# Top-k attention, SwiGLU and experts on one core: other staging rooms for the f64 weights, queries transposed unsplit, and routing in four batches

## The chip, the cores and the metric

The kernel runs on one core of a Trainium2 chip. The metric is device time in microseconds (us); lower is better. An engine is named as the profile names it: PE multiplies matrices (PEld loads its stationary operand), DVE is the vector engine, ACT the scalar engine, POOL the GpSimd engine, SP the queue from which most transfers are issued. PSUM holds what PE writes.

## The reference, cut to what matters

```python
# 1. attention, q k v: (4, 8, 576, 64) f32; only the 32 largest scores of a row count
scores = q @ k.T / 8
scores = where(scores >= kth_largest(scores, 32), scores, -1e9)
x = softmax(scores) @ v                      # -> 2304 tokens x 512
# 2. SwiGLU block; its three weight matrices come as 8-byte doubles
xn = x / rms(x) * rms_g
x = (silu(xn @ w_gate) * (xn @ w_val)) @ w_out          # 512 -> 1536 -> 512
# 3. one expert of eight per token
logits = x @ w_gate2 + modality_bias[modality_id]
e = argmax(logits); p = softmax(logits)[e]
out = p * (relu(x @ w1[e]) @ w2[e])                     # 512 -> 1024 -> 512
```

## The kernel before, in words

The program has two parts. `front` does attention, the SwiGLU block (called the MLP here) and the routing; then, after a short hand-over through DRAM, the experts run one after another. Nothing of the second part is touched.

**Attention** runs in 72 steps of two tiles (128 query rows against 576 keys each). In a step, PE multiplies q by k (`qk`, tile `ps`), DVE finds the 32nd largest of each row with repeated MAX8 and MATCH_REPLACE8 (`topk`, tile `w`), ACT and POOL make the softmax in place (tile `s`), PE transposes it (`tr`: tile `pt`, and once per step the 64 left-over keys of both tiles in tile `sm`) and multiplies by v (`av`). A number in f32 is carried as a pair, a rounded part and the rest ("hi" and "lo").

**The query path before.** `dma_q` loads the raw rows of a step into `qr` six steps ahead. `split_q`, four steps ahead, has POOL make the pair `qs` in two operations (L454, L455). `trans_q`, two steps ahead, has PE turn both parts of both tiles, four transposes of 128x128 (L463, tile `pq`), and ACT copies the result to `qS` in one go (L471, or L476 in the steps for left-over rows). `qk` of the step reads `qS`.

**The weights.** The doubles come in 36 chunks of 512 KB. A chunk is loaded raw, DVE turns it into f32 with three integer operations per piece (L277, L282, L286) in a PSUM tile `wp`, and ACT and POOL write the hi and lo halves into `wg`, `wv` or `wo` (L292 to L295). The 12 chunks of `w_out` come first and are staged in the still empty rooms of `wg` and `wv`. The 24 chunks of `w_gate` and `w_val` (columns in three parts, c0, c1 and c2, of eight chunks each) are staged in the ring of tag `h`, which holds three chunks at a time; a chunk's load waits until an older one is converted. The list `WS` names the step at which each chunk's conversion is written into the program: c0 at step 2, c1 at step 4, c2 at step 5. The `wp` tiles of these 24 come from the PSUM pool `ps_f`, which has two buffers and is also the MLP's.

**The MLP and the routing.** The 2304 tokens make 18 blocks of 128, grouped in 17 granules. When attention has finished a granule, `granule` gives its atoms: norm, transposes `px`, six products with `wg` and `wv` (48 matmuls each, tile `pf`), two with `wo` (36 each, tile `po`, with the routing logits in the last columns). `route` picks the expert of each token on DVE, and `rank` counts on PE (L866 to L868) and DVE at which place of its expert's list a token comes and scatters it there with POOL (L889): once per granule.

The order on each engine is set when the program is built: work is written in the order of the steps, and a scheduler with a model of the engines places each instruction; on the chip every engine runs its list strictly in order. SP, too, issues its transfers in list order, so a transfer that waits for its buffer holds those behind it.

## Time and profile before

| | before |
| --- | --- |
| median of 3 runs (range) | 1250.49 us (1248.81 to 1254.15) |
| the profiled execution | 1253.59 us |
| its span, first to last instruction | 1251.9 us |
| last `sm` transpose, end of attention on PE | 831.4 us |
| last product of the MLP | 929.2 us |
| first transpose of the experts | 948.3 us |

The span falls into four stretches: up to about 220 us the weights are converted beside attention; up to 831 us attention and MLP run together; up to 929 us PE works off the rest of the MLP; after a gap of 19 us the experts run to the end. "Busy" of PE is modelled from the starts of pipelined matmuls, so that a stretch at 99% is one in which PE always had something in flight.

### The profile page before, as it was taken

How to read it: one execution, taken by the hardware profiler on the slowest of the kernel's cores; microseconds unless marked ns; L12 is line 12 of the kernel's file. 1: busy time of each engine (PE TensorE's matmuls, PEld its weight loads, DVE VectorE, ACT ScalarE, POOL GpSimd, SP SyncE). 2: the span in 40 equal slices, each digit the busy share in tenths (PEclk: the TensorE clock that was granted, in tenths of full speed). 3: DMA queues.
4: the chain of work that ended last, by engine and by line, in shares of the span. 5: the costliest groups of instructions: out<-in, count | busy, mean ns of one | idle time of the engine just before them, and what ended most of it. 6: DMA issues, size and time to landing. Idle time of an engine off the chain costs nothing. (4 is left out here: it accounts for less than half of the span.)

```text
span 1251.9 us, 32217 instructions
## 1 busy us (share of the span) xinstructions
PE 1134.4 (91%) x12286; PEld 1038.2 (83%) x12286; DVE 925.4 (74%) x2885; ACT 832.3 (66%) x1757; POOL 736.2 (59%) x850
## 2 busy tenths in 40 slices
PE   6866777999999999999999999999975899999994
PEld 6855666888999999999899999999965789899893
DVE  8899999759999999999999999951214525454260
ACT  5868887777888888888888788763313535354260
POOL 7866766858767878876899667554325313221100
PEclk9866576989999999999999999999997899999997
DMA  9143312011000111100011000000007735553320
GB/s 292 51 128 83 98 43 81 13 44 39 20 17 11 33 37 47 26 9 17 20 32 42 25 17 2 11 11 11 10 21 263 264 113 189 185 186 102 103 87 19
DMA packets 68882, 87.63 MB, mean 70 GB/s; under 512 B 34386, under 2 KB 43734, under 8 KB 68696
## 3 DMA queue, kind: packets, MB, share of 16 engines
q1 hardware_dynamic: 60152, 63.66, 16.7%
q0 software_dynamic: 6320, 16.31, 3.9%
q10 hardware_dynamic: 2224, 5.25, 1.1%
q8 instruction: 109, 1.79, 0.6%
q14 instruction: 77, 0.63, 0.2%
HBM read 75.58 MB, written 10.92 MB: 69 GB/s over the span
## 5 line engine op out<-in xcount | busy, mean ns | idle before, releaser
L563 DVE MAX8 w<-w 128x8 f32<-128x296 f32 x576 | 249.9, 456 | 1.2
L597 POOL TENSOR_TENSOR s<-s,r 128x576 f32<-128x576 f32 x144 | 200.9, 1416 | 31.3 <-ACT r L593 31.1
L566 DVE MATCH_REPLACE8 w<-w 128x296 f32<-128x296 f32 x432 | 193.2, 450 | 0.0
L748 PE MATMUL pf<-xT,wg 128*128 128x128 f16 (+1 forms) x2448 | 172.0, 224 | 4.0 <-DVE T L877 2.6
L748 PE MATMUL pf<-xT,wv 128*128 128x128 f16 (+1 forms) x2448 | 167.7, 222 | 0.0
L528 PE MATMUL ps<-kS,qS 128*128 128x288 f32 x640 | 138.5, 346 | 24.1 <-DVE w L544 23.0
L748 PE MATMUL po<-wo,h 128*128 128x264 f16 (+1 forms) x1296 | 157.5, 275 | 0.9 <-ACT t L775 0.9
L748 PEld LDWEIGHTS <-wg 128*128 128x128 f16 x2448 | 148.2, 99 | 10.8 <-issue 4.6
L748 PEld LDWEIGHTS <-wv 128*128 128x128 f16 x2448 | 145.3, 98 | 4.3
L748 PEld LDWEIGHTS <-h 128*128 128x128 f16 x1296 | 122.0, 98 | 18.9 <-issue 1.4
L528 PEld LDWEIGHTS ps<-kS,qS 128*128 128x128 f32 x640 | 103.9, 215 | 27.4 <-ACT r L593 19.7
L1184 DVE SCALAR_TENSOR_TENSOR hl<-ph,hh 128x256 fp32r<-128x256 f32 x88 | 37.0, 421 | 117.9 <-ACT hh L1183 117.9
L1240 POOL DMA_INDIRECT out_dram<-o,idx x23 | 23.0, 1000 | 171.5 <-ACT o L1239 152.3
L601 ACT ACTIVATE s<-s,mbs 128x576 f32<-128x576 f32 x144 | 113.2, 788 | 14.0 <-POOL s L597 13.7
L593 ACT ACTIVATE r<-s,mbs 128x576 f32<-128x576 f32 x144 | 104.9, 779 | 18.3 <-POOL mbs L584 18.0
L623 PE MATMUL pt<-identr,s 128*128 128x128 f32 x576 | 98.4, 302 | 17.0 <-ACT s L601 15.8
L541 ACT COPY s<-ps 128x576 f32<-128x576 f32 x144 | 93.0, 646 | 23.6 <-PE ps L528 22.9
L1181 PE MATMUL ph<-xh,wh 128*128 128x256 f32 x352 | 100.2, 288 | 6.8 <-PEq L1293 6.3
L1181 PE MATMUL ph<-xl,wh 128*128 128x256 f32 x352 | 99.2, 283 | 0.0
L1181 PE MATMUL ph<-xh,wl 128*128 128x256 f32 x352 | 99.1, 283 | 0.0
L780 POOL TENSOR_TENSOR t<-u,t 128x512 f32<-128x512 f32 x54 | 70.5, 1305 | 48.0 <-ACT t L775 30.5
L669 PE MATMUL pt<-vs,pT 128*128 128x64 f16 (+1 forms) x1680 | 88.3, 198 | 7.5 <-POOL pT L637 5.8
(206 smaller groups left out, 2807.6 us busy)
## 6 DMA issues: line engine op xcount, KB each, us to landing
wr<-in_moe_w_dram SPq DMA_DIRECT2D x48, 512.0 KB
wst<-in_moe_w_gate_dram SPq DMA_DIRECT2D x24, 256.0 KB
wst<-in_moe_w_val_dram SPq DMA_DIRECT2D x24, 256.0 KB
wr<-in_moe_w_dram ACTq DMA_DIRECT2D x10, 512.0 KB
kr<-in_k_dram SPq DMA_DIRECT2D x32, 128.0 KB
vt<-in_v_dram SPq DMA_DIRECT2D x32, 128.0 KB
x_d<-xo SPq DMA_DIRECT2D x16, 256.0 KB
qr<-in_q_dram SPq DMA_DIRECT2D x112, 32.0 KB
```

Of the source, the lines that this page charges most:

```text
L528: nc.tensor.matmul(out=ps[:, a, 0:HS], lhsT=qS[i // 2][:, i % 2, j, o2:o2 + 128], rhs=kt[:, m, ks], start=(n == 0), stop=(n == len(ops) - 1),)
L541: nc.scalar.copy(out=s.rearrange("p (a k) -> p a k", a=2), in_=ps[:, :, 0:HS])
L563: steps.append(lambda: dve.max(lists[t][:, 8 * r:8 * r + 8], src[t] if r == 0 else dst[t]))
L566: steps.append(lambda: dve.match_replace(out=dst[t], in_to_replace=lists[t][:, 8 * r:8 * r + 8], in_values=src[t] if r == 0 else dst[t], i ...
L593: nc.scalar.activation(out=d["r"], in_=d["s"], func=AF.Relu, scale=-BIG, bias=d["mb"][:, 1:2])
L597: nc.gpsimd.tensor_tensor(out=d["s"], in0=d["s"], in1=d.pop("r"), op=OP.subtract)
L601: nc.scalar.activation(out=d["s"], in_=d["s"], func=AF.Exp, scale=SCALE, bias=d["mb"][:, 0:1], accum_out=d["rs"])
L623: nc.tensor.transpose(pt[:, c * 128:(c + 1) * 128], e[:, e0 + c * 128:e0 + (c + 1) * 128], ident)
L669: nc.tensor.matmul(out=av_[o:o + n], lhsT=l, rhs=r, start=(a == 0), stop=(a == len(ops) - 1))
L748: nc.tensor.matmul(out=out_, lhsT=l, rhs=r, start=(a == 0), stop=(a == len(ops) - 1))
L780: nc.gpsimd.tensor_tensor(out=t, in0=u, in1=t, op=OP.mult)
L1181: nc.tensor.matmul(out=pt, lhsT=l[:, fs], rhs=r[:, kk, :], start=(n == 0), stop=(n == 3 * KD - 1))
```

## The change

1. **Rooms.** The c0 chunks are staged in the parts of `wg` and `wv` that are meant for c1 and c2, as soon as `w_out` has left them. Five chunks of c1 are loaded before them, into the ring `h` (three), the MLP's `u` buffers and its `xT` buffer. Four more chunks go where c2 belongs, in four pieces each, and the last seven through the ring `h`. c0's `wp` tiles come from the pool `ps_t`, which is attention's. `WS` now has c0 at step 1, c1 at step 2 and c2 at step 3.
2. **Queries.** `dma_q` now comes four steps ahead and fills a wider `qr`, in which each raw row stands twice (the transfer repeats it). `split_q` is gone. PE turns the raw f32 tile, two transposes per step; ACT writes the rounded part into `qS` and a plain copy `qf`, and POOL subtracts, which gives the lo part of `qS`.
3. **Routing.** `route` and `rank` run four times, for 6, 6, 5 and 1 blocks, after granules 5, 10, 15 and 16 (counted from 0). Logits are collected in one tile per batch; `rank` counts within a batch with one more matmul per pair of blocks (40 in all, where one was).

```diff
+    ENDS = [NG // 3, 2 * NG // 3 - 1, NG - 2, NG - 1]
+    batches = [
+        [blk for g in range(lo + 1, hi + 1) for blk in granules[g][1]] for lo, hi in zip([-1] + ENDS[:-1], ENDS)
+    ]
...
+            elif i < KF + NC1:
+                r = third(1, 3, 2 * NC1)
...
+            elif i == KF + NC1 + 3:
+                ts = [mp.tile([128, WC // 2, 2], I32, name="wst", tag="u", bufs=UB) for _ in range(2)]
+            elif i == KF + NC1 + 4:
+                t = mp.tile([128, WC, 2], I32, name="wst2", tag="xT", bufs=1)
...
+            elif KF + NC1 + OWN <= i < KF + NC1 + OWN + 4:
+                r = third(2, 3, 16)
...
-            pool, tag = (ps_t, "pt") if i < KF else (ps_f, "f")
+            pool, tag = (ps_t, "pt") if i < KF + NC1 else (ps_f, "f")
...
-        WS, WAT = [-4] * 4 + [-1] * 8 + [2] * 8 + [4] * 8 + [5] * 8, -1
+        WS, WAT, W1 = [-4] * 4 + [-1] * 8 + [1] * 8 + [2] * 8 + [3] * 8, -1, 0
...
-            qr = ap_.tile([128, 2, D], F32, name="qr", tag="qr", bufs=QB)
+            qr = ap_.tile([128, 2, 2, D], F32, name="qr", tag="qr", bufs=QB)
...
+                    nc.sync.dma_start(out=qr[:, t], in_=src.unsqueeze(1).to_broadcast([128, 2, D]))
...
-            nc.gpsimd.tensor_tensor(out=qs[:, :, 0], in0=q2, in1=z, op=OP.add)
-            nc.gpsimd.tensor_tensor(out=qs[:, :, 1], in0=q2, in1=qs[:, :, 0].bitcast(F32), op=OP.subtract)
...
-            pt = ps_m.tile([128, 512], F32R, name="pq", tag="sm")
+            pt = ps_m.tile([128, 512], F32, name="pq", tag="sm")
             for t in range(2):
-                for j in range(2):
...
+                nc.tensor.transpose(
+                    pt[:, t * 128:(t + 1) * 128], qr[:, t].rearrange("p a d -> p (a d)"), ident
+                )
...
+                nc.scalar.copy(out=hi, in_=cut(src))
+                nc.scalar.copy(out=qf, in_=src)
+                nc.gpsimd.tensor_tensor(out=lo, in0=cut(qf), in1=hi.bitcast(F32), op=OP.subtract)
...
-                at(s - 6, lambda s=s: dma_q(s))
+                at(s - 4, lambda s=s: dma_q(s))
...
-            at(s - 4, lambda s=s: split_q(s))
...
-                        if j == nb - 1:
+                        if j == nb - 1 and gi in ENDS:
                             route()
...
-            return pre, hid, res, [rank()]
+            return pre, hid, res, [rank()] if gi in ENDS else []
```

On PE, where the MLP first gets long runs. Before, this is the piece after the 16th `sm` transpose; the last row is the first of 48 matmuls in a row (line numbers are those of the kernel before):

```order
L628 MATMUL sm<-identr,s 128x128
L423 MATMUL pk<-identr,ks 128x128
L669 MATMUL pt<-vt,pT 128x64 x8
L669 MATMUL pt<-vt,pr 128x64 x2
L463 MATMUL pq<-identr,qs 128x128 x4
L528 MATMUL ps<-kS,qS 128x288 x4
L419 MATMUL pk<-identr,ks 128x128 x4
L748 LDWEIGHTS wv_109
L748 MATMUL pf<-xT,wv_109 128x128
```

Now it is the piece after the 13th (lines are those of the changed kernel: L793 is the MLP's product, L667 `tr`, L490 the query transposes), and 47 matmuls with `wg` and 47 with `wv` follow:

```order
L572 MATMUL ps<-kS,qS 128x288 x4
L672 MATMUL sm<-identr,s 128x128
L490 MATMUL pq<-identr,qr 128x128 x2
L667 MATMUL pt<-identr,s 128x128 x8
L793 LDWEIGHTS wg_107
L793 MATMUL pf<-xT,wg_107 128x128
```

The MLP's first runs stand three steps earlier in PE's list. Up to the 72nd `sm` transpose PE's list holds 4847 of the 6192 MLP matmuls before and 5092 now.

On SP, the first transfers. Before, the queries of step 0 (`qr`) are third in the list:

```order
L264 DMA wg_107<-in_moe_w_out_dram 128x1024 x2
L373 DMA kr<-in_k_dram 128x256
L376 DMA kr<-in_k_dram 64x64
L373 DMA kr<-in_k_dram 128x256
L376 DMA kr<-in_k_dram 64x64
L443 DMA qr<-in_q_dram 128x64 x2
```

Now they come behind all of `w_out` and are followed by the loads of c1 and c0:

```order
L300 DMA wv_110<-in_moe_w_out_dram 128x1024 x2
L477 DMA qr<-in_q_dram 128x2x64 x6
L300 DMA wst<-in_moe_w_gate_dram 128x512 x8
L300 DMA wst_364<-in_moe_w_val_dram 128x512 x2
L300 DMA wg_107<-in_moe_w_gate_dram 128x512 x4
L300 DMA wg_108<-in_moe_w_gate_dram 128x512 x2
L411 DMA kr<-in_k_dram 128x256
L414 DMA kr<-in_k_dram 64x64
```

The first three steps' queries moved behind 12 chunks, and the third pair of key loads behind 16 weight pieces where it stood behind five.

On POOL, in the middle of attention, with `s<-s,r` the softmax and `t`, `h` the MLP. Before, each step has the two operations of `split_q`:

```order
L597 TENSOR_TENSOR s<-s,r 128x576 x2
L454 TENSOR_TENSOR qs<-qr,zero 128x2x128
L637 TENSOR_TENSOR pT<-pf,pT 128x512
L407 TENSOR_TENSOR ks<-kr,zero 128x9x64
L455 TENSOR_TENSOR qs<-qr,qs 128x2x128
L780 TENSOR_TENSOR t<-u,t 128x512
```

Now it has one, which needs PE's transposes and both of ACT's copies first (L641 is the softmax, L825 and L827 the MLP):

```order
L628 TENSOR_TENSOR mbs<-w,cst_66 128x6
L509 TENSOR_TENSOR qS<-qf,qS 128x2x128
L641 TENSOR_TENSOR s<-s,r 128x576 x2
L509 TENSOR_TENSOR qS<-qf,qS 128x2x128
L825 TENSOR_TENSOR t<-u,t 128x512
L651 TENSOR_SCALAR sums<-sums 128x2
L827 TENSOR_TENSOR h<-t,h 128x512
```

The operation moved from ahead of the transposes to between them and `qk`. Between the last query transpose of a step and its first `qk` matmul, PE's list now holds 3 to 320 matmuls, in the middle 150; 11 of the 72 steps have fewer than 40.

## Rows read from the trace of the kernel before

**Rows 1.** Page, its first part and the granted clock (busy us, share, count).

```profile
PE 1134.4 (91%) x12286; PEld 1038.2 (83%) x12286; DVE 925.4 (74%) x2885; ACT 832.3 (66%) x1757; POOL 736.2 (59%) x850
...
PEclk9866576989999999999999999999997899999997
```

**Rows 2.** Busy time by stretch: PE, PEld, DVE, ACT, POOL, granted clock, DMA share, GB/s.

```profile
0.00:30.00 30.00, 18.49 (x115) 17.90 (x116) 24.16 (x53) 18.29 (x36) 22.93 (x42) 1.00 0.92 296
100.00:150.00 50.00, 33.87 (x201) 28.56 (x200) 50.00 (x167) 40.24 (x85) 35.98 (x41) 0.57 0.32 88
150.00:200.00 50.00, 37.17 (x299) 32.59 (x299) 50.00 (x171) 42.16 (x91) 34.96 (x45) 0.71 0.22 63
300.00:825.00 525.00, 520.35 (x6987) 481.21 (x6988) 508.15 (x1744) 435.81 (x978) 402.82 (x472) 1.00 0.08 23
350.00:800.00 450.00, 447.05 (x6017) 413.45 (x6016) 433.88 (x1479) 377.20 (x847) 345.39 (x402) 1.00 0.09 24
```

**Rows 3.** The chain of waits, its first piece: start us, us, what.

```profile
1205.87 0.97 DMA out_dram<-o,idx
```

**Rows 4.** Timeline of PE: `sm` transposes 13, 16, 72 (start us, us, engine, line).

```profile
179.23 0.33 PE L628 MATMUL sm<-identr,s 128*128 128x128 f32 x1
...
219.82 0.35 PE L628 MATMUL sm<-identr,s 128*128 128x128 f32 x1
...
831.41 0.28 PE L628 MATMUL sm<-identr,s 128*128 128x128 f32 x1
```

**Rows 5.** Timeline of DVE: a converted piece and what follows it at once.

```profile
219.29 0.42 DVE L277 TENSOR_SCALAR wp<-wst 128x256 int32<-128x256 int32 x1
219.62 0.42 DVE L286 SCALAR_TENSOR_TENSOR wp<-wst,wp 128x256 int32<-128x256 int32 x1
...
5.31 0.69 DVE L282 SCALAR_TENSOR_TENSOR wp<-wg,wp 128x512 int32<-128x512 int32 x1
5.92 0.69 DVE L277 TENSOR_SCALAR wp<-wg 128x512 int32<-128x512 int32 x1
```

**Rows 6.** Timeline of PE after attention: dense runs of the MLP.

```profile
911.68 2.84 PE L748 MATMUL pf<-xT,wg 128*128 128x128 f16 x48
...
917.04 10.72 PE L748 MATMUL po<-wo,h 128*128 128x264 f16 x95
```

**Rows 7.** Groups of PE in 350 to 800 us: out<-in xcount, busy us, mean ns.

```profile
L748 PE MATMUL pf<-xT,wg 128*128 128x128 f16 (+1 forms) x1385 | 103.6, 225 | 2.4 <-DVE u L770 1.1 <-DVE T L877 0.9 <-ACT t L775 0.3
L748 PE MATMUL pf<-xT,wv 128*128 128x128 f16 (+1 forms) x1344 | 98.8, 225 | 0.0
L748 PE MATMUL po<-wo,h 128*128 128x256 f16 (+1 forms) x762 | 94.5, 275 | 0.0
L628 PE MATMUL sm<-identr,s 128*128 128x128 f32 x42 | 11.7, 278 | 0.0
```

**Rows 8.** Timeline of PE: runs of query and of softmax transposes at granted clock 1.00.

```profile
286.77 0.26 PE L463 MATMUL pq<-identr,qs 128*128 128x128 f32 x1
286.92 0.45 PE L463 MATMUL pq<-identr,qs 128*128 128x128 f32 x3
...
232.25 0.61 PE L623 MATMUL pt<-identr,s 128*128 128x128 f32 x4
281.80 1.04 PE L623 MATMUL pt<-identr,s 128*128 128x128 f32 x8
```

**Rows 9.** Groups of the whole span: transposes, copies and POOL operations.

```profile
L463 PE MATMUL pq<-identr,qs 128*128 128x128 f32 x288 | 43.2, 272 | 1.5 <-ACT qS L471 1.3 <-ACT kS L422 0.2
L623 PE MATMUL pt<-identr,s 128*128 128x128 f32 x576 | 98.4, 302 | 17.0 <-ACT s L601 15.8 <-ACT xn L678 0.8
L471 ACT CAST qS<-pq 128x512 fp32r<-128x512 f32 x64 | 39.2, 613 | 1.5 <-PE pq L463 1.4
L812 ACT ACTIVATE xo<-po 128x256 f32<-128x256 f32 x36 | 13.8, 388 | 26.9 <-DVE L L807 20.8 <-PE po L748 6.0
L454 POOL TENSOR_TENSOR qs<-qr,zero 128x256 fp32r<-128x256 f32 x72 | 44.4, 616 | 32.4 <-PE pq L463 31.5 <-PE pk L419 0.6
L455 POOL TENSOR_TENSOR qs<-qr,qs 128x256 fp32r<-128x256 f32 x72 | 52.5, 730 | 2.3
L597 POOL TENSOR_TENSOR s<-s,r 128x576 f32<-128x576 f32 x144 | 200.9, 1416 | 31.3 <-ACT r L593 31.1
```

**Rows 10.** Timeline of one routing after attention, DVE and PE (brackets: idle time, releaser).

```profile
902.46 0.16 DVE L840 TENSOR_REDUCE mx<-L 128x1 f32<-128x8 f32 x1
...
903.60 0.15 DVE L855 TENSOR_SCALAR gt<-gt 128x1 f32<-128x1 f32 x1
...
906.03 0.16 DVE L884 TENSOR_TENSOR acc_oh<-acc_oh,O 128x8 f16<-128x8 f16 x1 [1.25 <-PE pr L868]
...
906.83 0.14 DVE L887 COPY pay<-gt 128x1 f32<-128x1 f32 x1
...
906.32 2.84 PE L748 MATMUL pf<-xT,wg 128*128 128x128 f16 x48 [0.33 <-DVE T L877]
...
831.58 0.17 PE L867 MATMUL pr<-acc_oh,ones 128*128 128x8 f16 x1
831.61 0.17 PE L868 MATMUL pr<-O,tri 128*128 128x8 f16 x1
```

**Rows 11.** The first 30 us: SP and DVE timeline; DMA queue: packets, MB, share.

```profile
4.05 1.06 SPq L443 DMA_DIRECT2D qr<-in_q_dram  x2
...
14.83 2.50 SPq L264 DMA_DIRECT2D wv<-in_moe_w_out_dram  x5
...
19.04 0.45 DVE L543 TENSOR_TENSOR w<-s,ps 128x288 f32<-128x288 f32 x1
...
q1 hardware_dynamic: 60152, 63.66, 16.7%
```

**Rows 12.** Groups of the whole span: POOL's scatter of the routing.

```profile
L889 POOL DMA_INDIRECT tab_d<-pay,si x18 | 19.2, 1068 | 14.0 <-DVE pay L887 11.9 <-issue 1.4 <-DVE w L545 0.3
```

More of the change, by code (lines that the diff above doesn't have):

```diff
@@ L249, in weight_chunk, with third @@
             return src, [t[:, kk, cs] for t in (wg_sb, wv_sb)[which]], (g_sb if exact else gs_sb)[:, kk:kk + 1]
+        NC1 = 2 * KD
+        OWN = 5
+        def third(c0, c1, n):
+            u = DM * (2 if not exact else 4) // 4
+            rows = [
+                t.bitcast(I32)[:, kk, c0 * u:c1 * u].rearrange("p (f t) -> p f t", t=2)
+                for t in wg_sb + wv_sb for kk in range(KD)
+            ]
+            k = max(n // len(rows), 1)
+            w = rows[0].shape[1] // k
+            return [r[:, a * w:(a + 1) * w] for r in rows for a in range(k)]
         def load_weights(i):
@@ L262, in load_weights @@
             n = WC // len(ts)
+            assert all(t.shape[1] == n for t in ts)
             for a, t in enumerate(ts):
@@ L354, in front @@
         WA, WQ = 6, 0
-        WX = [-5] * 4 + [-2] * 8 + [1] * 8 + [3] * 8 + [4] * 8
+        WX = [-5] * 4 + [-2] * 8 + [1] * 8 + [2] * 8 + [3] * 8
         MS, HP, HQ = 0, 500, 0
@@ new lines, in dma_q @@
+            for t, (b, p, hh, c) in enumerate(steps[s]):
+                if hh is not None:
+                    src = q[b, 2 * p + hh, 0:SM, :].rearrange("(p c) d -> p c d", c=CM)[:, c, :]
+                    nc.sync.dma_start(out=qr[:, t], in_=src.unsqueeze(1).to_broadcast([128, 2, D]))
+                else:
+                    for i in range(2):
+                        src = q[b, 2 * p + i, SM:S, :]
+                        nc.sync.dma_start(
+                            out=qr[i * SR:(i + 1) * SR, t], in_=src.unsqueeze(1).to_broadcast([SR, 2, D])
+                        )
@@ L691, in granule @@
             G = 512 // n
+            bi, batch = next((i, bl) for i, bl in enumerate(batches) if blocks[0] in bl)
             x = [xn.pop(j) for j in blocks]
@@ L843, in route @@
                 if not exact:
-                    d = new("d", [2, E])[:, 0:nb]
+                    d = new("d", [NBM, E])[:, 0:nr]
                     nc.vector.tensor_tensor(out=d, in0=L, in1=L, op=OP.subtract)
@@ L847, in route @@
                     nc.vector.tensor_reduce(
-                        out=finite[:, gi:gi + 1], in_=d.rearrange("p j e -> p (j e)"), axis=AX.X, op=OP.min
+                        out=finite[:, bi:bi + 1], in_=d.rearrange("p j e -> p (j e)"), axis=AX.X, op=OP.min
                     )
@@ L862, in pe @@
                     O = rt["O"]
-                    for j in range(nb):
+                    for j in range(nr):
                         o = pt[:, j * E:(j + 1) * E]
```

128 lines of the change are left out of this document (69 added, 59 removed).

## The prediction

> **What bounds the kernel now.** I read the page first: PE is busy 91% of the span, DVE 74% [rows 1], an average over stretches with different limits. The chain of waits begins at 1205.87 us [rows 3] and says nothing of the part that changes, so the stretches decide [rows 2]. From 100 to 200 us DVE is busy in every microsecond while PE has work for two thirds of the time, at a granted clock of 0.57 and 0.71, that is, between its two levels of 1.2 and 2.4 GHz: here DVE sets the pace, with the 32nd-largest search and the conversion of the weights. From 300 to 825 us PE is busy 520.35 of 525 us at full clock and DVE 508.15: PE is the limit, DVE just under it. After the last `sm` transpose at 831.4 us [rows 4] PE has the rest of the MLP to itself up to 929 us. So PE is full from about the 16th `sm` transpose, at 219.8 us [rows 4], to 929 us, and what comes after (323 us of experts) is untouched. The change is worth what it takes out of that full stretch, and what PE work it moves in front of it, where PE stands idle.
>
> **Prices.** A dense run of 48 matmuls of `pf` takes 2.84 us and 95 of `po` 10.72 us [rows 6]: 0.059 and 0.113 us each, so 0.070 us in the mix of a granule (288 and 72). In 350 to 800 us PE is busy 447 us [rows 2], with 2729 `pf`, 762 `po` and 42 `sm`, so 42 steps [rows 7]. The MLP is 2729 x 0.059 + 762 x 0.113 = 247 us of it; 200 us are left, 4.75 us of PE per attention step. Taking the MLP's busy time as the groups give it (297 us) leaves 3.6 us, the lower bound.
>
> **1. Rooms: the MLP starts three steps earlier.** In PE's list the first long MLP run moves from behind the 16th `sm` to behind the 13th, which before stood at 179.2 us [rows 4]. It will not stand there again, since DVE, the limit in that stretch, now has all conversions in front of it. Up to its 13th step DVE's list has 72 conversion operations more than before, 24 of 256 and 48 of 128 columns. Operations of 256 and 512 columns follow each other at 0.33 and 0.61 us [rows 5], which puts 128 columns at 0.19 (an estimate on that line): 24 x 0.33 + 48 x 0.19 = 17 us. By durations (0.42 and 0.69, so 0.29) it is 24 us. I take 18, near the starts, because DVE had no gaps there. So PE becomes full at 197 us instead of 219.8, 22.6 us earlier; but three steps of attention, 14.3 us of PE work, are then still to do, and 46 MLP matmuls (2.7 us) that PE had slipped in before. Net gain 5.6 us, bounds 0 and 10. The same ledger says that attention ends about when it did, near 831 us, with 245 more MLP matmuls behind it, and that the rest after it is shorter by 17 us.
>
> **2. Queries.** Three of four query transposes in a row start 0.095 us apart ((0.45 - 0.26) / 2), the f32 softmax ones 0.108 us ((1.04 - 0.61) / 4) [rows 8]. The new ones are of the second kind: 4 x 0.095 - 2 x 0.108 = 0.165 us less per step, over the 59 steps in PE's full stretch 9.7 us. Bounds: busy time per transpose, 43.2 / 288 = 0.150 against 98.4 / 576 = 0.171 [rows 9], gives 2 us if the new ones cost 0.171 each but the old only 0.095, and 18 us if half of 0.150 x 4 goes.
>
> ACT gets two copies of 256 columns (0.388 each, by the row of that width) for one of 512 (0.613) [rows 9]: 0.16 x 72 = 12 us more on an engine that is busy 436 of 525 us [rows 2]. POOL loses 0.616 x 72 = 44 us [rows 9]. Neither is on the path; I cost them at nothing. Between a step's transposes and its `qk` now lie 0.39 + 0.39 + 0.73 = 1.5 us instead of 0.61; the built order has some 150 matmuls (10 us) there to hide them, but fewer than 40 in 11 steps. I take +1 us, bounds 0 and 10 (11 x 0.9).
>
> The repeated rows add 18,432 pieces of 256 B. At the mean packet's price, 16.7% of 16 engines' span over 60,152 packets = 0.056 us [rows 11], that is 64 us on one sixteenth of a system that is at 8% in the full stretch [rows 2]: nothing. It may matter only in the first 30 us, where the DMA share is 0.92 [rows 2]: six tiles, 768 pieces, 768 x 0.056 / 16 = 2.7 us by packets, 0.7 us by bytes (0.2 MB at 296 GB/s). The Trainium skill, in "DMA: Bandwidth & Descriptors", section Specifications, sets at least 512 B for a transfer at line rate and says that below it an engine reads and writes back, which speaks against this part. By that rule the 2.7 would hold, without it the 0.7; no row separates 256 B pieces, so no run here shows which, and both lie inside the next term.
>
> **3. The start.** The queries of step 0 were issued at 4.05 us and the search began at 19.0 us, between conversions [rows 11]. Now they stand behind all 12 chunks of `w_out`, issued to 17.3 us [rows 11]; 6.3 MB at 296 GB/s [rows 2] have landed near 23 us, the last two chunks take DVE 6 x 0.61 us more, and the search begins near 28 us. By then DVE had done some 4 us of it. Behind that come 2.6 MB of c1 ahead of c0, 9 us at that rate, while DVE has a step's search to do first. I take 3 us lost, bounds 0 (DVE also stood idle 5.8 of these 30 us [rows 2]) and 10.
>
> **4. Routing.** After attention a routing holds PE for 0.33 us [rows 10]; 13 fewer are 4.3 us, less 39 counting matmuls more, which start 0.03 us apart [rows 10]: 3.1 us gained, bounds 0 and 5. On DVE one takes 1.3 + 0.9 us [rows 10], 13 of them 29 us. DVE is not the limit, but at 97% it sometimes delays PE; with POOL's relief I take 4 us, bounds 0 and 25 (rival A). POOL's scatters come in rows: five at 1.07 us [rows 12] in the last granule, 5.3 us, beside 17 us of `pf` runs that hide them; without that cover 3 us.
>
> **Sum:** -5.6 - 9.7 + 1 + 3 - 3.1 - 4 = -18.4 us, from the profiled execution's 1253.6 us to 1235. The median of the runs is 3.1 us lower than that execution, so I forecast 1232 us; its own range, with bounds that rarely fall on one side together, is 1218 to 1245.
>
> **Rivals.** *A, DVE is the true pace.* PE's busy time is modelled and may hide gaps in which it waits for DVE's result. For: DVE at 97%, few gaps on either [rows 2]. Against: idle time on PE put down to DVE is 2 us in the `pf` groups [rows 7]. If so, 25 of the 29 us (11 of the 13 routings end during attention) come back, 0.45 us per step out of attention's 4.75: 1232 + 4 - 25 = 1211 us.
>
> *B, the earlier start is lost.* SP issues in order; c0 waits for the rooms of `w_out`, the key loads stand behind 16 weight pieces, and DVE, also in order, waits at the first piece that is late. Then term 1 is 0 and term 3 is 10: 1232 + 5.6 + 7 = 1245 us, no change that can be told. For: the start is limited by transfers [rows 2]. Against: rooms for 13 chunks instead of three.
>
> *C, slower: the new subtraction holds PE.* POOL runs in order, and a softmax operation of 1.42 us [rows 9] just ahead makes the path from transposes to `qk` 2.9 us, about 40 matmuls. Where fewer lie between, PE stands, and with it everything. For the 11 short steps that is 32 us: 1232 + 32 = 1264 us; it decides from about seven of them on. If POOL ran late everywhere it would be far more. Against: POOL is busy 403 of 525 us [rows 2] and loses work.
>
> **How the numbers follow.** Chances: forecast 0.58, A 0.18, B 0.16, C 0.08. The range leaves out half of A and nearly all of C: 1210 to 1252. About 0.5% (6 us) is what a measurement of this kernel can tell from no change. Faster by more (below 1244): most of the forecast, A and a third of B, 0.73; within it 0.17, mostly B; slower 0.10, C and the forecast's upper end.
>
> **What would show it.** Term 1: PE's first long MLP runs near 197 us, and some 1100 instead of 1345 MLP matmuls after the last `sm`. Term 2: 144 query transposes, started 0.1 us apart. Term 3: the first search operation near 28 us. Term 4: 4 routings, DVE's share in 300 to 825 us lower by 5 points while PE's stays. It would be wrong if PE's busy share in the full stretch fell with attention no faster (C), if DVE showed idle time on a weight piece before 150 us (B), or if attention ended well before 831 us (A).

## The result: 1263.9 us, 1% slower

The changed kernel takes 1263.94 us (median of 4 runs, 1260.50 to 1266.18) against 1251.84 us (4 runs, 1248.81 to 1254.15) of the kernel before: a ratio of 1.0098, 95% interval 1.0076 to 1.0119. The forecast was 1232 us, its range 1210 to 1252. The profiled execution has a span of 1258.9 us, 7.0 more than before, and the page answers [rows 1]:

```profile
PE 1130.4 (90%) x12181; PEld 1028.7 (82%) x12181; DVE 918.1 (73%) x2678; ACT 832.7 (66%) x1816; POOL 693.3 (55%) x778
...
PEclk9996558999999999999999998999997899999997
```

Less work on PE, DVE and POOL, and a longer time. So the added time is waiting, or work at a lower clock. The stretches, in the columns of [rows 2]:

```profile
0.00:30.00 30.00, 17.39 (x104) 16.01 (x105) 23.94 (x43) 19.83 (x41) 20.92 (x35) 1.00 0.94 317
100.00:150.00 50.00, 38.07 (x201) 32.77 (x202) 50.00 (x187) 40.28 (x89) 29.25 (x33) 0.53 0.09 23
300.00:825.00 525.00, 513.83 (x6822) 471.54 (x6820) 488.21 (x1539) 428.91 (x999) 369.41 (x418) 0.99 0.12 30
350.00:800.00 450.00, 440.38 (x5825) 403.24 (x5825) 416.64 (x1313) 368.54 (x859) 319.74 (x359) 0.99 0.12 29
```

In the stretch where PE was the limit it is idle 11.2 us instead of 4.7, and its clock is no longer 1.00. DVE has 20 us less to do there, and the kernel gains nothing by it. The `sm` transposes 13 and 72, as in [rows 4]:

```profile
199.54 0.27 PE L672 MATMUL sm<-identr,s 128*128 128x128 f32 x1
...
851.72 0.27 PE L672 MATMUL sm<-identr,s 128*128 128x128 f32 x1
```

The 13th stands at 199.5 us, where the forecast put it (197). The 72nd, forecast near 831, stands at 851.7. That place alone is no measure of a loss, since the order also decides how much of the MLP stands ahead of it (with the new rooms alone, an experiment below, it stands at 850.2 us in a kernel of 1249.1); what PE loses in each stretch is counted further down.

**Where PE stops.** The second batch of the routing, on POOL (start us, us; in brackets the idle time ahead and what ended it):

```profile
741.30 1.07 POOL L942 DMA_INDIRECT tab_d<-pay,si  x1 [0.65 <-PE pf L793]
...
745.71 1.01 POOL L942 DMA_INDIRECT tab_d<-pay,si  x1 [1.94 <-DMA tab_d<-pay,si]
746.73 2.79 POOL L641 TENSOR_TENSOR s<-s,r 128x576 f32<-128x576 f32 x2
749.68 0.99 POOL L942 DMA_INDIRECT tab_d<-pay,si  x1 [0.17 <-issue]
...
753.10 1.01 POOL L942 DMA_INDIRECT tab_d<-pay,si  x1 [0.84 <-DMA tab_d<-pay,si]
754.13 1.18 POOL L827 TENSOR_TENSOR h<-t,h 128x512 f16<-128x512 f32 x1
757.43 0.99 POOL L942 DMA_INDIRECT tab_d<-pay,si  x1 [2.12 <-DVE w L607]
758.45 1.17 POOL L681 TENSOR_TENSOR pT<-pf,pT 128x512 f16<-128x512 f32 x1
759.56 0.73 POOL L509 TENSOR_TENSOR qS<-qf,qS 128x256 fp32r<-128x256 f32 x1
760.81 0.99 POOL L942 DMA_INDIRECT tab_d<-pay,si  x1 [0.52 <-DMA tab_d<-pay,si]
```

and PE at the same place:

```profile
756.00 0.60 PE L772 MATMUL px<-identr,xn 128*128 128x128 f32 x4
759.67 0.50 PE L713 MATMUL pt<-vs,pT 128*64 128x64 f16 x10 [3.08 <-POOL pT L681]
```

Six scatters write one table, `tab_d`, and the program lets each wait until the one before has landed, that is, until its data is written: they start 3.4 to 4.4 us apart, not 1.07, and take from 741.3 to 761.8 us. (The Trainium skill, in "DMA: Bandwidth & Descriptors", section "Two DMAs through the same engine are not ordered", says that a transfer that depends on an earlier one is ordered only by that one's completion signal, on which the issuing engine has to wait; the brackets of three of the five later scatters name that landing.) The other two: that of 749.68 had its landing at 748.4 us and was held by the softmax operations ahead of it, and that of 757.43 is put down to DVE, but the landing before it is recorded at 757.16 us, and it starts 0.27 us later, as the other three do after theirs (0.26 or 0.27). POOL runs its list in order, so `pT`, which PE waits for, stands behind a scatter that stands behind a transfer; what `pT` reads was ready at 754.6 us, when ACT had written `pf`, and it starts at 758.45. The clock falls on top of that; the stretch 740 to 775 us, in the columns of [rows 2], before and now:

```profile
740.00:775.00 35.00, 34.97 (x535) 32.57 (x533) 33.13 (x108) 27.55 (x62) 23.17 (x27) 1.00 0.04 12
740.00:775.00 35.00, 31.21 (x364) 27.14 (x363) 26.79 (x91) 21.31 (x49) 23.63 (x26) 0.90 0.05 9
```

Now PE is 3.8 us idle, and the mean granted clock is 0.90, which is 10% of 35 us of work at full clock: 7.3 us in all. The third batch does the same in the last granule, where `t` and `h` of the MLP stand between the scatters:

```profile
915.83 1.01 POOL L942 DMA_INDIRECT tab_d<-pay,si  x1 [1.88 <-DMA tab_d<-pay,si]
919.24 0.97 POOL L942 DMA_INDIRECT tab_d<-pay,si  x1 [2.40 <-DMA tab_d<-pay,si]
920.23 1.28 POOL L825 TENSOR_TENSOR t<-u,t 128x512 f32<-128x512 f32 x1
923.09 1.01 POOL L942 DMA_INDIRECT tab_d<-pay,si  x1 [1.58 <-DMA tab_d<-pay,si]
924.12 1.17 POOL L827 TENSOR_TENSOR h<-t,h 128x512 f16<-128x512 f32 x1
```

The chain to PE goes over ACT and DVE (the next ACT operation is the `u` that this DVE operation needs):

```profile
921.54 0.62 ACT L826 CAST h<-t 128x512 f16<-128x512 f32 x1 [6.21 <-POOL t L825]
...
922.76 0.69 DVE L815 SCALAR_TENSOR_TENSOR u<-u,pf 128x512 f32<-128x512 f32 x1 [9.32 <-ACT u L814]
...
923.50 2.91 PE L793 MATMUL po<-wo,h 128*128 128x264 f16 x18 [3.51 <-DVE u L815]
```

PE's wait is put down to DVE, DVE's to ACT, ACT's to POOL's `t` of 920.23, and that stood behind the scatter of 919.24 and its landing. The group of the scatters, as in [rows 12], had 14.0 us of idle time ahead of it, none of it put down to a landing; now:

```profile
L942 POOL DMA_INDIRECT tab_d<-pay,si x18 | 18.4, 1022 | 22.4 <-DMA tab_d<-pay,si 10.2 <-DVE pay L940 8.2 <-DVE w L607 2.1
```

**One measure for all kernels.** To compare places, I give each PE matmul a price, the lower sixth, over all kernels, of the times from a start of its kind to the next start (kind: operands, shape, what follows). What a stretch takes beyond the sum of its prices is lost, by idle time or by the lower clock. Stretches are bounded by the `sm` transposes 13, 22, 36, 41, 61 and 66 and the last MLP matmul. The rows below the second are the experiments that follow. In the kernels with batches the first stands in 36 to 41, the second in 61 to 66 and the third behind 66.

| PE's lost us | to 13 | 13-22 | 22-36 | 36-41 | 41-61 | 61-66 | 66-end | sum | median us |
|---|---|---|---|---|---|---|---|---|---|
| before | 100.5 | 43.9 | 8.7 | 6.1 | 11.1 | 3.4 | 5.7 | 179.4 | 1251.8 |
| changed | 120.4 | 16.0 | 10.3 | 7.3 | 9.8 | **10.2** | **10.6** | 184.6 | 1263.9 |
| rooms alone | 124.3 | 14.6 | 10.1 | 5.3 | 14.4 | 5.4 | 6.2 | 180.3 | 1249.1 |
| queries alone | 101.8 | 37.5 | 10.7 | 7.5 | **17.9** | 3.9 | 6.4 | 185.7 | 1260.9 |
| routing alone | 101.1 | 36.6 | 9.2 | **10.7** | 9.9 | **8.8** | **10.1** | 186.4 | 1256.0 |
| rooms and queries | 119.1 | 18.9 | 8.8 | 3.0 | 14.9 | 2.9 | 5.1 | 172.7 | 1249.8 |
| changed, spread | 117.5 | 14.4 | 8.3 | 7.7 | 9.7 | 3.4 | 3.6 | 164.6 | 1243.2 |
| trains without batches | 117.1 | 14.6 | 7.3 | **10.1** | 12.5 | **5.5** | **8.1** | 175.2 | 1251.4 |
| spread, added trains, one table | 118.6 | 16.6 | 12.2 | 7.8 | 9.9 | **6.8** | **11.2** | 183.1 | 1252.6 |
| spread, added trains, six tables | 120.4 | 18.3 | 10.2 | **13.3** | 9.0 | **10.1** | **8.3** | 189.6 | 1260.6 |
| spread, added scatters spread | 116.2 | 14.6 | 8.3 | 7.6 | 10.8 | 4.8 | 7.8 | 170.1 | 1237.9 |

PE's priced work up to there differs by under 6 us among them. A loss is not passed on to the end exactly: from the last MLP matmul to the end it is 315 to 323 us, so totals and losses can differ by 8 us.

### The profile page after: what moved, and what is told of

Its sections match the earlier page's. It is cut to its first block, busy times and chain, and to the rows that moved or that the text cites. A ratio compares the mean times of both kernels' runs of the same rounds, so it can differ in the third digit from the quotient of the medians.

```text
span 1258.9 us, 31800 instructions
## 1 busy us (share of the span) xinstructions
PE 1130.4 (90%) x12181; PEld 1028.7 (82%) x12181; DVE 918.1 (73%) x2678; ACT 832.7 (66%) x1816; POOL 693.3 (55%) x778
## 3 DMA queue, kind: packets, MB, share of 16 engines
q1 hardware_dynamic: 80888, 68.38, 17.9%
## 5 line engine op out<-in xcount | busy, mean ns | idle before, releaser
L607 DVE MAX8 w<-w 128x8 f32<-128x296 f32 x576 | 252.5, 460 | 2.8
L641 POOL TENSOR_TENSOR s<-s,r 128x576 f32<-128x576 f32 x144 | 201.5, 1419 | 49.2 <-ACT r L637 47.8
L793 PE MATMUL pf<-xT,wv 128*128 128x128 f16 (+1 forms) x2448 | 174.7, 222 | 0.0
L793 PE MATMUL pf<-xT,wg 128*128 128x128 f16 (+1 forms) x2448 | 169.7, 222 | 1.0 <-DVE acc_oh L931 0.6
L793 PE MATMUL po<-wo,h 128*128 128x264 f16 (+1 forms) x1296 | 161.2, 278 | 6.7 <-DVE u L815 3.5
L572 PE MATMUL ps<-kS,qS 128*128 128x288 f32 x640 | 141.8, 346 | 21.8 <-DVE w L588 17.8
L793 PEld LDWEIGHTS <-wg 128*128 128x128 f16 x2448 | 147.4, 98 | 7.1 <-issue 1.3
L793 PEld LDWEIGHTS <-wv 128*128 128x128 f16 x2448 | 148.8, 98 | 5.2
L793 PEld LDWEIGHTS <-h 128*128 128x128 f16 x1296 | 124.5, 99 | 27.1 <-issue 7.5
L645 ACT ACTIVATE s<-s,mbs 128x576 f32<-128x576 f32 x144 | 114.2, 798 | 18.3 <-POOL s L641 18.0
L667 PE MATMUL pt<-identr,s 128*128 128x128 f32 x576 | 99.3, 300 | 20.9 <-ACT s L645 11.2
L637 ACT ACTIVATE r<-s,mbs 128x576 f32<-128x576 f32 x144 | 105.0, 780 | 14.7 <-POOL mbs L628 14.5
L713 PE MATMUL pt<-vs,pT 128*128 128x64 f16 (+1 forms) x1680 | 91.1, 198 | 12.4 <-POOL pT L681 6.9
L667 PEld LDWEIGHTS pt<-identr,s 128*128 128x128 f32 x576 | 71.9, 154 | 28.5 <-ACT s L645 17.7
```

Source lines behind the costliest of these rows:

```text
L572: nc.tensor.matmul(out=ps[:, a, 0:HS], lhsT=qS[i // 2][:, i % 2, j, o2:o2 + 128], rhs=kt[:, m, ks], start=(n == 0), stop=(n == len(ops) - 1),)
L607: steps.append(lambda: dve.max(lists[t][:, 8 * r:8 * r + 8], src[t] if r == 0 else dst[t]))
L637: nc.scalar.activation(out=d["r"], in_=d["s"], func=AF.Relu, scale=-BIG, bias=d["mb"][:, 1:2])
L641: nc.gpsimd.tensor_tensor(out=d["s"], in0=d["s"], in1=d.pop("r"), op=OP.subtract)
L645: nc.scalar.activation(out=d["s"], in_=d["s"], func=AF.Exp, scale=SCALE, bias=d["mb"][:, 0:1], accum_out=d["rs"])
L667: nc.tensor.transpose(pt[:, c * 128:(c + 1) * 128], e[:, e0 + c * 128:e0 + (c + 1) * 128], ident)
```

## Experiments: each part alone

Theory R: the trains of scatters are the loss. Theory S: the later start is. Each kernel below is timed against the kernel before in its own series (medians 1250.4 to 1252.4 us).

**The rooms alone** (label rooms): the weights' part of the diff, nothing else.

```diff
-        WS, WAT = [-4] * 4 + [-1] * 8 + [2] * 8 + [4] * 8 + [5] * 8, -1
+        WS, WAT, W1 = [-4] * 4 + [-1] * 8 + [1] * 8 + [2] * 8 + [3] * 8, -1, 0
...
```

> The weights' rooms and the times of their loads and conversions as in the changed kernel; queries and routing as before. The forecast's first term said -5.6 us (0 to -10) for this alone, so about 1246. Theory S (the loss of the changed kernel lies in its start: first search 29.5 us against 19.0, transposes of the early steps 15 to 27 us later): if the rooms are what brings the late start, this kernel shows it too, is 1258 or more, and its 13th sm transpose stands near 199 us. Theory R (the loss lies in the routing trains): this kernel is at 1246 to 1250, and nothing of it stalls at 756 us.

Measured: 1249.07 us, ratio 0.9985 (0.9964 to 1.0006). Up to the 22nd step PE loses 138.9 us instead of 144.4: as much less as the forecast's 5.6 us. But the queries alone and the routing alone, which leave the rooms as they were, lose 139.3 and 137.7 there, so this pair by itself doesn't show that the rooms do it. After that it loses 6.4 us more than before, in places that the rooms don't touch; what is left in the total cannot be told from nothing. Nor is there a late start to see: the first search is at 19.3 us.

**The queries alone** (label queries): loads, transposes and subtraction of the diff.

```diff
-            at(s - 4, lambda s=s: split_q(s))
             at(s - 2, lambda s=s: trans_q(s))
...
-                at(s - 6, lambda s=s: dma_q(s))
+                at(s - 4, lambda s=s: dma_q(s))
```

> Only the queries as in the changed kernel (raw rows, two f32 transposes a step, subtraction behind the eviction, loads four steps ahead instead of six). The forecast's second term said -9.7 us for the tiles, so about 1243 with a start 1 to 3 us later. From the trace of the changed kernel the saving is only 0.11 us a step (the start after the transposes, on the first sm, rose from 43 to 104 ns), 6.7 us over 59 steps: 1245. Theory S: if the queries' later loads bring the late start, the first search here is near 28 us and the kernel is at 1252 to 1260. Theory R: 1243 to 1247.

Measured: 1260.89 us, ratio 1.0077 (1.0055 to 1.0100): slower, 0.9 us above even the range of S. The first search stands at 30.3 us, as S had it, but by the 22nd step PE has lost less than before. The loss is in 56 to 61 (9.9 us against 2.6), on POOL at an ordinary routing of one granule each:

```profile
713.92 1.07 POOL L885 DMA_INDIRECT tab_d<-pay,si  x1 [2.96 <-DVE pay L883]
...
718.50 0.99 POOL L885 DMA_INDIRECT tab_d<-pay,si  x1 [2.88 <-DVE w L540]
719.51 1.17 POOL L633 TENSOR_TENSOR pT<-pf,pT 128x512 f16<-128x512 f32 x1
```

and on PE:

```profile
720.73 0.47 PE L665 MATMUL pt<-vs,pT 128*128 128x64 f16 x10 [1.82 <-POOL pT L633]
```

The new order had put the scatters ahead of `pT`. (The second is put down to DVE; the landing of the first is recorded at 718.23 us, 0.27 us before it starts.)

**The routing alone** (label route): batches, no other change (one buffer of `pay` instead of two, for room).

```diff
-                        if j == nb - 1:
+                        if j == nb - 1 and gi in ENDS:
                             route()
```

> Only the routing in four batches; weights and queries as before. Theory R (six scatters of a batch, each waiting for the landing of the one before and holding GpSimd in order, stall the attention and drop the clock; 7.7 us between the 66th and the 71st step of the changed kernel, beyond those more at the other batches): this kernel is 6 to 12 us slower, 1258 to 1264. Theory S and the forecast's fourth term: 0 to -25 us, about 1245 to 1252, since the start is untouched.

Measured: 1255.96 us, ratio 1.0034 (1.0017 to 1.0050). Slower, below R's range by 2 us; PE loses 4.6, 5.4 and 4.4 us more than before at the three batches, and wins 7 back in 13 to 22, ahead of its first batch. At the first two it is the same wait as above, 3.2 and 2.3 us for POOL's `pT`.

**Rooms and queries** (label rooms_queries), the changed kernel with the old routing (`T2` in the buffer of `T`, for room).

```diff
-                        if j == nb - 1 and gi in ENDS:
+                        if j == nb - 1:
                             route()
...
```

> The changed kernel with the routing of before, one a granule. Theory R: 1264 less 8 to 12 us, so 1252 to 1256, and the steps from the 66th to the 71st keep their distance to the kernel before. Theory S: 1260 to 1266, as the changed kernel, with the first search near 29 us. If neither of the parts alone is slower and this one is, the loss is in how the two together are dealt into the order.

Measured: 1249.78 us, ratio 0.9992 (0.9972 to 1.0011). That is 2 us below the range of R. S falls: the first search is at 29.3 us and 14 us of the loss are gone. The late start is not what costs; the routing is, in this company. And the queries with their later start, on top of the rooms, bring 0.7 us the wrong way, which is no difference that can be told.

## Experiments: the scatters' places

**Spread** (label after_spread): the changed kernel; a batch's scatters are kept and put one by one behind every second `h<-t,h` of the MLP. Two rivals of R are set against it: V, that the batch itself costs (its longer block of work on DVE), and N, that any new order of the program moves the time as much.

```diff
                     for j in range(nr):
-                        nc.gpsimd.indirect_dma_start(
+                        spill.append(lambda j=j: nc.gpsimd.indirect_dma_start(
...
+                        if spill and (turn[0] % 2 == 0 or gi == NG - 1):
+                            with tc.issue_after(behind.ins):
+                                spill.pop(0)()
```

> The changed kernel, still routed in four batches, but a batch's scatters stand one by one behind every second GpSimd product of the MLP (one each in the last granule) and no longer as a train of six. Theory R (the trains' scatters, each waiting for the landing of the one before while GpSimd's other work stands behind them, are the loss: PE loses 4.2 to 7.3 us more per batch than without batches, 16 us in all): 1248 to 1253, and no step between the 36th and the last loses PE more than 5 us. Rival V (the batch itself is the loss: its block on VectorE of six tokens' blocks at once, the one product list for all, the later finite flag): it stays at 1260 to 1266. Rival N (any new order of the built program moves the time by this much): anything from 1245 to 1265.

Measured: 1243.23 us, ratio 0.9920 (0.9892 to 0.9947): faster than both kernels, 5 us below the range of R, and 20.7 us under the changed one. Batches two and three lose 6.8 and 7.0 us less, about 14 us together; the other 6 us are 2 to 3 us in each of the first three stretches, ahead of any scatter, so they are the new order's and not the trains'. Batch one had cost nothing in the changed kernel. The wait for a landing is not by itself a loss of PE's: the scatters of this kernel wait 8.2 us for one, too, but all at the end (909.7 to 920.1 us), where POOL has no MLP product left behind them. The stretch that answers the one above, no gap and full clock:

```profile
740.00:775.00 35.00, 35.00 (x479) 32.02 (x477) 32.48 (x102) 28.91 (x69) 23.52 (x28) 1.00 0.08 21
```

V falls as the whole cause, since the batch's block on DVE is all there.

**Closer spread** (label after_spread1): behind every product instead of every second.

```diff
-                        if spill and (turn[0] % 2 == 0 or gi == NG - 1):
+                        if spill:
```

> The changed kernel with its scatters behind every GpSimd product of the MLP instead of every second, so some 12 us apart. Nothing should wait for a landing at that distance, so by theory R it is at the time of the kernel with every second, 1243, and what it differs is what a new deal of the order is worth: 1239 to 1249. If the distance mattered beyond the landing, it would lose 3 us or more at each of the batches.

Measured: 1244.17 us, ratio 0.9936 (0.9913 to 0.9959). As R said; and a new order, dealt by the scheduler, is worth 1 us here.

**Trains without batches** (label rq_train): rooms and queries, one routing a granule, scatters held and issued six at a time.

```diff
+                        if len(spill) >= 6 or gi == len(granules) - 1:
+                            with tc.issue_after(behind.ins):
+                                while spill:
+                                    spill.pop(0)()
```

> The kernel with the new rooms and queries and one routing a granule (1249.8 us), but the scatters are held back and issued in trains of six at the places where the four batches stood; VectorE's routing stays as before, one a granule. Theory R: the trains alone bring the loss, 10 to 16 us: 1260 to 1266. Rival V: 1248 to 1253, since the batch's block on VectorE is not there.

Measured: 1251.41 us, ratio 0.9992 (0.9978 to 1.0006). By the total R misses, by 9 us, and V's number comes. By place PE loses 10.1, 5.5 and 8.1 us in 36 to 41, 61 to 66 and behind 66 where rooms and queries lost 3.0, 2.9 and 5.1, that is 12.7 us more, and 10 less elsewhere, where nothing was changed but the order. But 7.1 of the 12.7 stand at the first train, where PE's waits are put down to DVE and not to POOL:

```profile
511.14 0.78 PE L707 MATMUL pt<-vs,pT 128*128 128x64 f16 x12 [2.65 <-DVE pT L677]
```

At the second train POOL waits 2.9 us for landings where the changed kernel waits 5.4, since more of its other work fell between the scatters, and PE loses 5.5 us where that loses 10.2. So this run leaves 5.6 us at most to the trains: the loss goes with the waiting, but trains without batches cost next to nothing, and why it takes both is not shown.

**Two controls.** The kernel with the queries alone, its scatters behind the next product (label queries_spread), and the kernel before with the same (label before_spread), by the edit of the closer spread.

> The kernel with the new queries alone (1260.9 us), each granule's one or two scatters standing behind the next GpSimd product of the MLP. There PE lost 7.5 us between the 56th and the 61st step, where GpSimd stood 5.9 us at two scatters for their payload. Theory R in its wider form (a scatter that stands too early in GpSimd's list holds the attention): 1252 to 1256, the rest above 1250 being its late start. Rival N: the place is gone but another comes up, 1252 to 1264.

Measured: 1254.97 us, ratio 1.0032 (1.0012 to 1.0053). The gap in 56 to 61 is gone (2.4 us) and 5.9 us with it: R in its wider form.

> The kernel before, with nothing changed but the scatters' places (behind the next GpSimd product of the MLP), which deals the whole order anew: 41,000 of 45,000 rows of TensorE's list stand elsewhere. It says what a new deal alone is worth. Theory R: no scatter waited long in the kernel before, so 1250 to 1254. Rival N: 1245 to 1265, and then differences under about 8 us between such kernels say nothing of their parts.

Measured: 1253.95 us, ratio 1.0014 (0.9999 to 1.0030). The same work in a wholly new order: 2 us, though single stretches differ by 5 to 7. So totals that differ by 2 or 3 us say nothing of their parts, and a single stretch needs a wait in the trace beside it; the 20.7 us between the changed kernel and the spread one are far beyond that.

**The wait or the closeness?** Kernels with added trains of scatters into spare tables that nobody reads, on top of the spread kernel: one table for all (label dum_same), six tables, so that none waits for another (label dum_apart), six tables and the added ones spread too, one scatter behind every product (label dum_far).

```diff
+                    for j in range(nr):
+                        nc.gpsimd.indirect_dma_start(
+                            out=dum[j], out_offset=bass.IndirectOffsetOnAxis(ap=si[:, j:j + 1], axis=0),
...
```

(`dum[0]` in the first of the three.)

> The changed kernel with its scatters spread (1243.2 us), and added to it at the four batches a train of scatters, one for each block, with the same data into one spare table that nobody reads: each has to wait for the landing of the one before, as the trains of the changed kernel had. Theory R (the wait for the landing, in GpSimd's list ahead of the attention's work): PE loses 10 to 16 us more around the 41st and the 66th step and at the end, so 1253 to 1259. Rival Q (only the scatters' own 1.07 us each, on GpSimd or as traffic, count): 0 to 6 us, 1243 to 1249.

> The same added trains, but each scatter of a train goes into a spare table of its own, so none waits for another; the number of scatters, their bytes and their issue are those of the kernel with one spare table. Theory R: the loss is all but gone, 1243 to 1248 (six times 1.07 us of GpSimd in a row at a batch). Rival Q: the same loss as with one spare table.

> The changed kernel with its scatters spread, and as many again into spare tables that nobody reads, but each of them, too, behind a GpSimd product of the MLP of its own, so that none stands close to another before the last granule. Same number of scatters and bytes as in the kernels with added trains (1252.6 us and 1260.6 us). If closeness is what costs: 1243 to 1248. If the number of scatters costs: 1252 or more.

Measured: 1252.61 us (ratio 1.0003, 0.9987 to 1.0019), 1260.55 (1.0062, 1.0038 to 1.0086) and 1237.93 (0.9896, 0.9847 to 0.9944), the last 5 us below the lower of its two ranges. The number of scatters costs nothing in the total: with twice as many, all apart, the kernel is at least as fast as without. (PE loses 5.5 us more than in the spread kernel, 170.1 for 164.6; from the last MLP matmul to the end this kernel takes 316.6 us and the spread one 323.2, so up to 5 us may be hidden there.) Closeness costs 9 us in the total where each waits for a landing, 0.4 us less than R's range. But without any such wait it costs 17, where R said 5 at most: R's wait is one way to the loss, not the only one. With six tables POOL starts a scatter every 1.3 us:

```profile
498.77 0.97 POOL L947 DMA_INDIRECT dum<-pay,si  x1 [0.30 <-issue]
500.05 0.97 POOL L947 DMA_INDIRECT dum<-pay,si  x1 [0.30 <-issue]
501.32 0.97 POOL L947 DMA_INDIRECT dum<-pay,si  x1 [0.30 <-issue]
```

and PE, whose products there wait for no operand, runs on beside the first of them; from 500.8 us it starts one product at a time, until 505.0:

```profile
499.89 0.86 PE L794 MATMUL pf<-xT,wg 128*128 128x128 f16 x10
502.13 0.22 PE L794 MATMUL pf<-xT,wg 128*128 128x128 f16 x1 [1.38 <-issue]
503.55 0.27 PE L794 MATMUL pf<-xT,wg 128*128 128x128 f16 x1 [1.21 <-issue]
504.30 0.27 PE L794 MATMUL pf<-xT,wg 128*128 128x128 f16 x1 [0.48 <-issue]
505.03 0.60 PE L794 MATMUL pf<-xT,wg 128*128 128x128 f16 x4 [0.46 <-issue]
```

"issue" is time in which the engine waited for nothing that the profile shows. Over the span that is, in one group of PE:

```profile
L794 PE MATMUL pf<-xT,wg 128*128 128x128 f16 x2304 | 157.4, 221 | 9.8 <-issue 8.9 <-DVE acc_oh L936 0.7 <-ACT t L821 0.3
```

In the changed kernel the group of the same name has 1.0 us of idle time and none at "issue". So there it is the landing and POOL's order; what holds PE in the kernel with six tables stays open. No packet of the two instruction queues (q8, q14) moves between 495.1 and 507.7 us in its trace, so a late piece of program is not seen to end these gaps.

## Experiments: the queries, the start, the batches

**The queries' worth without trains** (label rr_spread): the spread kernel with the old queries (and one buffer of `pay`).

```diff
-            pt = ps_m.tile([128, 512], F32, name="pq", tag="sm")
+            pt = ps_m.tile([128, 512], F32R, name="pq", tag="sm")
...
```

> The changed kernel with its scatters spread, but with the queries as before (split to a rounded and a rest part by GpSimd, four transposes a step). The forecast's second term said the new queries are worth 9.7 us: then this is at 1253. By the groups of TensorE's instructions in the runs so far they are worth 2 us (four transposes at 95 ns gone for two at 110, but the start after the transposes of sm 67 ns and that of the score products 5 ns a piece later): 1242 to 1248.

Measured: 1248.66 us, ratio 0.9968 (0.9952 to 0.9984), so the queries are worth 5.4 us here and -0.7 between the two kernels without batches. Both pairs hold the later start as well (first search at 20.0 and 29.5 us here), so they answer to the forecast's second and third terms together, 9.7 - 1 - 3 = 5.7 us. What the transposes alone bring is seen in PE's timeline. Rooms alone:

```profile
402.12 0.60 PE L665 MATMUL pt<-identr,s 128*128 128x128 f32 x4
402.56 0.27 PE L670 MATMUL sm<-identr,s 128*128 128x128 f32 x1
402.59 0.53 PE L495 MATMUL pq<-identr,qs 128*128 128x128 f32 x4
402.97 0.23 PE L790 MATMUL pf<-xT,wg 128*128 128x128 f16 x1
```

Rooms and queries:

```profile
404.88 0.61 PE L661 MATMUL pt<-identr,s 128*128 128x128 f32 x4
405.33 0.27 PE L666 MATMUL sm<-identr,s 128*128 128x128 f32 x1
405.44 0.38 PE L484 MATMUL pq<-identr,qr 128*128 128x128 f32 x2
405.65 0.50 PE L786 MATMUL pf<-xT,wg 128*128 128x128 f16 x6
```

From `sm` to the `pf` behind the queries it is 0.41 us with four and 0.32 with two. The two raw ones are started 0.11 us apart, as forecast, but the `sm` ahead of them, which took 0.03 us to the next start, now takes 0.11 as well. Over the 49 steps from the 22nd to the 71st `sm`, start to start: `pq` 17.8 us to 10.8, `sm` 2.0 to 5.4, `ps` 66.6 to 69.7. Of 7.0 us won, 6.5 are given back; between the two spread kernels it is 18.8 to 10.4, 2.5 to 5.2 and 67.0 to 68.5, half of it. The part of `sm` comes back in every kernel with the new queries (4.7 to 5.4 us, with the old ones 2.0 to 3.1); that of `ps` overlaps (67.4 to 72.0 and 66.6 to 68.2) and may be the order.

**The start** (label early_q): the spread kernel with the first three steps' queries loaded as early as before.

```diff
-                at(s - 4, lambda s=s: dma_q(s))
+                at(s - (6 if s < 3 else 4), lambda s=s: dma_q(s))
```

> The changed kernel with its scatters spread, and the first three steps' queries loaded six steps ahead, as in the kernel before, so that they stand ahead of most of the output weights in the transfer queue. The first search comes near 20 us instead of 29.5. If the later start costs what the forecast's third term or rival B took (3 to 10 us): 1233 to 1240. If the rooms make the start one of transfers and conversions in any order, as the equal TensorE loss by the 22nd step of the kernels with the rooms alone and with rooms and queries says: 1241 to 1246.

Measured: 1239.83 us, ratio 0.9916 (0.9874 to 0.9958), beside 0.9920 without it. The first search is back where it was,

```profile
18.88 0.44 DVE L587 TENSOR_TENSOR w<-s,ps 128x288 f32<-128x288 f32 x1
```

and up to the 22nd step PE loses 137.4 us, against 131.9. So the 10.5 us at the first search are not seen on PE. By the total they are not settled: 1239.8 us lies in the range that was given for a start that costs, and 3.4 us below the spread kernel, but the five runs go from 1235 to 1247, and beside the kernel before in its own series the ratio is the same within 5 us.

**The batches' worth** (label route_spread): the kernel with the routing alone, its scatters spread by the same edit.

```diff
+                        if spill and (turn[0] % 2 == 0 or gi == NG - 1):
...
```

> The kernel before with the routing in four batches (1256.0 us as trains), the scatters spread. The forecast's fourth term said -7.1 us without the trains (TensorE -3.1, VectorE -4): 1245. If only the trains' removal counts: 1250 to 1253.

Measured: 1248.29 us, ratio 0.9986 (0.9963 to 1.0008): 7.7 us under the same kernel with trains, and 2 under the kernel before. On top of rooms and queries the spread batches, the new places of the scatters included, are worth 6.5 us (1249.78 to 1243.23). The forecast's 7.1 is the upper end.

## Why the prediction was wrong, point by point

- **Term 1, the rooms (-5.6).** Right in mechanism and place: the 13th `sm` at 199.5 us and PE's first long MLP run at 200.7 (197.8 with the rooms alone) for 197. Its size is only made likely: up to the 22nd step the kernels of the table with the new rooms lose 130.8 to 138.9 us, those without 137.7 to 144.4, about 5 us less in the mean, but the ranges overlap. And it did not reach the end: with the rooms alone attention ends at 850.2 us, not near 831, with 265 more MLP matmuls done, the last MLP matmul starts at 928.6 us for 929.0, and the total is 3.3 us shorter, which is no difference that can be told.
- **Term 2, the queries (-9.7 and +1).** Mis-sized on PE: `pq` itself won the forecast's 0.165 us a step (7.0 to 8.4 us in 49 steps, where that makes 8.1), but 2.7 to 3.4 us of it went back. It priced the four that go and the two that come, each by runs of its own kind, and not the start behind `sm` ahead of them (0.03 to 0.11 us). Its worth in the total isn't measured alone: with term 3 it is +0.7 to -5.4 us, where the two were forecast at -5.7. The pieces of 256 B cost more than their bytes, and less than the mean packet that the prediction went by. The queue's row, 60,152 packets and 63.66 MB in 16.7% [rows 11], is now

```profile
q1 hardware_dynamic: 80888, 68.38, 17.9%
```

  and the prediction's "no row separates 256 B pieces" holds for its rows, not for the traces: by their records of single packets one of 256 B takes 0.018 us on its engine, before (22,528 of them) as now (43,008), and not 0.056. That is 14.5 GB/s, where those of 2048 B move 19.7 and 20.6. The Trainium skill ("DMA: Bandwidth & Descriptors", Specifications) asks for at least 512 B for line rate and says that below it the engine reads, modifies and writes; the lower rate agrees with the first, no run shows the second. That the pieces cost the kernel time is not seen, with the DMA engines at 12% in the full stretch.
- **Term 3, the start (+3).** The first search at 29.5 us for 28: right. Its price is not shown: with the search back at 18.9 us PE loses 5.5 us more up to the 22nd step, not less, and the total (early_q) can't tell 3 us from nothing.
- **Term 4, routing (-7.1).** PE's and DVE's part held, as an upper end (-2 to -6.5). **The step that failed** is its last: "POOL's scatters come in rows: five at 1.07 us [rows 12] in the last granule, 5.3 us, beside 17 us of `pf` runs that hide them; without that cover 3 us." It priced a scatter by its own duration, where a train of six into one table ran at the pace of its landings, 20 us; and it looked at the last granule alone, where two of the trains stand in the attention, in one list with `pT`, `t` and `h`. What it cost at nothing cost about 14 us at the second and third batch; the 20.7 us between the changed kernel and the spread one hold 6 more that stand ahead of any scatter. The trace had the hint: in the kernel before, all scatters but one pair (712.5 and 716.7 us) start 21 us or more apart, and the change put them side by side.
- **Rival C** named the engine and the size, 1264 us by POOL's list holding PE, but the wrong instruction. The subtraction on POOL was to hold `ps`, and `ps` hardly waits at all, and not for POOL, in 300 to 825 us:

```profile
L572 PE MATMUL ps<-kS,qS 128*128 128x288 f32 x436 | 87.1, 320 | 1.7 <-DVE w L588 1.3 <-PE pt L713 0.4
```

  What the prediction named as its sign, PE's busy share falling with attention no faster, is what came, but for another reason. A falls: DVE has 20 us less, and even with the scatters spread the kernel is at 1243 us, not 1211. B falls by place: up to the 22nd step the changed kernel loses 8.0 us less than the kernel before, not more.
- **The sum.** By the totals, one part after another: rooms -3.3, queries and start +0.7, batches without trains -6.5, trains +20.7 (some 14 by place, and 6 of order), together +11.6; measured +12.1. They add up because each kernel is compared with the one before it in this row, so the sum proves nothing; and each part has 2 or 3 us of luck with the order in it.

## What to carry over

Before you gather small jobs into one big one, ask what the last of each does, not only what the bulk costs: transfers that write one table, each made to wait for the one before, ran here at the pace of their landings, and on an engine that works in order everything behind them waited as well. Issue them one by one, each behind work of its own, and the gain of the gathering stays (1243 us, where as a train it was 1264). And where a scheduler deals the order, compare stretches and look for the wait in them: a total carries some microseconds from places that nobody touched, and so does a stretch.

## What was not expected of the hardware

- Scatters of 128 rows of 8 bytes into one table, each made to wait for the landing of the one before, started 3.4 to 4.4 us apart, for 1.0 us of their own.
- Beside the last three of six scatters without a wait between them, 1.3 us apart, PE got one product at a time and was idle at "issue" (1.38, 1.21, 0.48 us); with such trains added the time rose by 17 us. The cause is open.
- An f32 transpose of 128 columns is followed by another f32 one after 0.11 us, but by a rounded (fp32r) one after 0.03, the next then 0.14 later: what stands behind an instruction sets its price.
- After 3.08 us without work on PE, the granted clock was 0.66 from 760 to 770 us, so in part at the lower of its two levels.
